# A stated task order in place of a greedy list scheduler, in a fused recurrent-attention and feed-forward kernel

## The chip, the core and the metric

The kernel runs on one core of a Trainium2 chip. The metric is the device time of the whole program in microseconds; three runs are shown for the kernel before, and beside them one profiled execution whose records the rows below come from. In the records PE is TensorE, DVE is VectorE, ACT is ScalarE, POOL is GpSimd and SP is SyncE, which issues all loads and stores.

## The reference

The first half is a gated linear recurrence over 768 steps for 4 batches and 8 heads of 48 columns; the second is a feed-forward block on the result, with token shift, squared ReLU and a sigmoid gate. Everything is float32.

```python
f = 1 / (1 + exp(-f_logit))
for t in range(S):                       # per batch and head; state is D x D
    state = f[t, :, None] * state + outer(k[t], v[t])
    y[t] = q[t] @ state
x = y, heads side by side                # (B, S, 384)
xk = mu_k * x + (1 - mu_k) * x_prev      # x_prev: x shifted by one step
xr = mu_r * x + (1 - mu_r) * x_prev
k = relu(xk @ w_k);  v = (k * k) @ w_v;  r = sigmoid(xr @ w_r)   # 384 -> 1024 -> 384
out = r * v
```

## The kernel before

The recurrence is cut into 24 chunks of 128 steps (N; six per batch), the feed-forward block into 8 units of three chunks (U). Every piece of work is a task with a short name, and the program is a list of tasks. For chunk i they are: loads `qk` and `v` (SP); `b`, a scan on DVE that multiplies the gates up; `bl`, its last column; `ln` and `rb` (ACT), the reciprocal; `q`, `n`, `kr`, `k`, which scale queries and keys; `TR`, four transposes of k on PE, and `kt`, their copy out of PSUM; `SP`, 32 small matmuls for the scores and then up to 32 for the state sums; `m`, the mask on the scores (for chunk 0 a copy on ACT, then `mg` on POOL); `g`, `za`, `zb`, `T`, which carry the state; `YA` and `YB`, the output matmuls, with `w`, a short wait between them; and `y`, the copy of the result into x.

For unit u they are: `sp` (six small transfers that spread two heads over free partitions of x), `x0`, `d`, `xm`, `xh`, `xl` (token shift, then the split of a float32 into a high part and a remainder, for keys n=0 and gate n=1 and three row blocks each); `F`, eight groups of nine matmuls with w_k; `r`, `h`, `kk`, `l` (ReLU, square, and its split); `R`, three groups of nine with w_r; `lg` and `sg` (the gate); `W`, six groups of twelve with w_v; `o` and `out`. All 1,368 matmuls of F, R and W are on line 505, and each product is made of three. `F0.0` needs `xl0.00` to `xl0.02`; every F, R and W follows the one before it.

The weights come as 64-bit words in 18 pieces (8 of `wk`, 4 of `wr`, 6 of `wv`), and each is turned into float32 by three DVE instructions (`S`, `T`, `X` at lines 623, 634 and 637), a cast on ACT (`H`) and a subtraction (`L`). Later the pieces are read once more for a check (`c`, `cm`, then `lo`, `lot`, `lom`, `strong`), which chooses a general path that does not run on these inputs.

PSUM holds four rotating buffers `pm`, which b, TR, d, F, R, W and the weights' S share, and two fixed tiles: `pss` for scores and sums, `py` for outputs. SBUF buffers rotate too (`BUFS`).

What sets the order: `Plan.schedule` is a greedy list scheduler. It runs on the host when the program is built; every task has a guessed duration for each engine that may take it, a `place` (a due time), and a DMA has a guess of its own. In turn it takes the task that can start first, and emits it; `emit` pins each engine's instructions to that order, so every engine works strictly down its list. Where PE would be without work by the guesses, after an early part, `fill` puts in small matmuls of the identity into an unused part of `py` (line 702). Constants hold some work back: `TIED` and `BUNDLE` keep YA behind the next chunk's kt and q, and YB behind the next chunk's SP; `late` and `behind` hold loads; `DEAR` makes DVE and ACT look dearer than POOL where there is a choice.

```python
near = I("kt", i + 1) + I("q", i + 1) + I("m") + I("T") if BUNDLE and TIED <= i < N - 1 else []
pl.add(f"SP{i}", at, ("P", 0.8 if cs < NCH - 1 else 0.62, 0, scores_sums),
       after=I("q") + I("kt") + I("m", i - 1) + I("zb", i - 1) + I("T", i - 1), uses=[("ktk", i), ("v", i)])
```

Of the kernel before, what the change touches and what calls it, by code (L numbers as in the profile page):

```python
# [59 lines left out]
class Plan:  # L60

    def __init__(self):
        self.tasks, self.users = {}, defaultdict(list)
        self.filler = None

    def add(self, name, place, *ways, after=(), takes=(), uses=()):
        assert name not in self.tasks, name  # L70
# [12 lines left out]

    def schedule(self, trace=None):
        free = {"P": 0.0, "V": 2.2, "A": 0.0, "G": 1.0, "Q": 0.7}
        wire, under = 0.0, [0.0] * 8
        last_p = "F"
        read = 0.0
        end, slot = {}, {}
        slots = {tag: [(0.0, i) for i in range(n)] for tag, (n, _) in BUFS.items()}  # L90
        left = {b: len(u) for b, u in self.users.items()}
        last = defaultdict(float)
        waits = {n: set(t[3]) for n, t in self.tasks.items()}
        for b, us in self.users.items():
            taker = [n for n in us if b in self.tasks[n][4]]
            assert len(taker) == 1, (b, taker)
            for n in us:
                if n != taker[0]:
                    waits[n].add(taker[0])
        then = defaultdict(list)  # L100
        for n, w in waits.items():
            for m in w:
                assert m in self.tasks, (n, m)
                then[m].append(n)
        ready = {n: () for n, w in waits.items() if not w}
        way_of = {}
        order = []
        while ready:
            best = None
            for n, names in ready.items():  # L110
                _, place, ways, _, takes, _ = self.tasks[n]
                at = 0.0
                if any(not slots[b[0]] for b in takes):
                    continue
                for b in takes:
                    at = max(at, min(slots[b[0]])[0])
                at = {w[0]: max([at] + [0.0 if way_of[m] == w[0] else end[m] for m in names]) for w in ways}
                pick = min(((max(at[w[0]], free[w[0]]) + w[1] + DEAR.get(w[0], 0.0), w) for w in ways), key=lambda x: x[0])[1]
                start = max(at[pick[0]], free[pick[0]])
# [2 lines left out]
                if best is None or k < best[0]:
                    best = (k, n, start, pick)
            assert best, "no order: " + ", ".join(sorted(ready))
            _, n, start, way = best
            _, _, _, _, takes, uses = self.tasks[n]
            e, us, port, _ = way
            if e == "P" and self.filler and "cst" in end:

                t = max(free["P"], read, FILL[0])  # L130
                stop = t + (start - t - 0.25) * FILL[1]
                cold = t + 6.0 if last_p == "F" else 0.0
                while t + (us4 := 1.76 if t < cold else 0.88) < stop:
                    name = f"fill{len(order)}"
                    fw = "P", 0.88, 0, lambda: self.filler(4)
# [1 line left out]
                    order.append((name, fw, slot))
                    if trace is not None:
                        trace.append((name, "P", t, t + us4))
                    free["P"] = t = t + us4  # L140
                    last_p = "FILL"
            if e == "Q":

                for _ in range(port):
# [802 lines left out]
```

## Time and profile before

| | |
|---|---|
| three runs | 359.09, 359.39, 360.88 us (median 359.39) |
| span of the profiled execution, first to last instruction | 361.0 us |
| PE busy | 329.9 us, 4514 matmuls |
| DVE busy | 262.8 us, 528 instructions |
| ACT busy | 200.3 us |
| POOL busy | 195.0 us |
| DMA | 45.32 MB |

The profiled execution has no time of its own beside the span, so the span is set against the runs directly: it is 1.6 us above their median. Busy time is a sum over the whole span; what an engine waits for is read from a stretch. In the records one instruction's end can overlap the next one's start on the same engine, so a sum over a queue is better made from start to start.

### The profile page before, as it was taken

How to read it: one execution, taken by the hardware profiler on the slowest of the kernel's cores; microseconds unless marked ns; L12 is line 12 of the kernel's file. 1: busy time of each engine (PE TensorE's matmuls, PEld its weight loads, DVE VectorE, ACT ScalarE, POOL GpSimd, SP SyncE). 2: the span in 40 equal slices, each digit the busy share in tenths (PEclk: the TensorE clock that was granted, in tenths of full speed). 3: DMA queues.
4: the chain of work that ended last, by engine and by line, in shares of the span. 5: the costliest groups of instructions: out<-in, count | busy, mean ns of one | idle time of the engine just before them, and what ended most of it. 6: DMA issues, size and time to landing. Idle time of an engine off the chain costs nothing.

```text
span 361.0 us, 10931 instructions
## 1 busy us (share of the span) xinstructions
PE 329.9 (91%) x4514; PEld 315.1 (87%) x4514; DVE 262.8 (73%) x528; ACT 200.3 (55%) x398; POOL 195.0 (54%) x235
## 2 busy tenths in 40 slices
PE   0496689988999999999999999999999999999993
PEld 0385589878989999999999999999999989999993
DVE  7979668989988988986998678948964852733210
...
PEclk9999667999999999999999999999999999999998
...
GB/s 283 405 334 190 246 142 82 83 107 129 182 185 137 27 117 285 165 200 183 245 139 49 141 193 165 0 50 95 105 80 36 50 26 6 14 44 22 3 24 51
DMA packets 20650, 45.32 MB, mean 126 GB/s; under 512 B 2928, under 2 KB 13040, under 8 KB 20592
## 3 DMA queue, kind: packets, MB, share of 16 engines
q1 hardware_dynamic: 20592, 44.55, 37.6%
q8 instruction: 37, 0.61, 0.7%
...
## 4 chain that ended last, share of the span: by engine, by line
PE 84%; DVE 7%; POOL 2%; issue 2%; DMA 2%; ACT 1%; DVEq 0%; ACTq 0%
PE pm L505 64%; PE py L362 8%; PE pss L325 4%; PE pm L310 4%; PE py L702 3%; PE pss L345 3%; DVE pm L240 2%; DMA words<-in_wv 1%; DVE pm L634 1%; POOL wk L644 1%; DVE pm L623 1%; DMA lg<-in_wr 1%; POOL wv L644 1%; DVE qk L250 1%; POOL k2l L543 1%
## 5 line engine op out<-in xcount | busy, mean ns | idle before, releaser
L505 PE MATMUL pm<-xh,wk 128*128 128x384 f32 x384 | 105.2, 345 | 1.6 <-POOL wk L644 1.4
L505 PE MATMUL pm<-wv,k2h 128*128 128x384 f32 x384 | 98.8, 338 | 0.0
L543 POOL TENSOR_TENSOR k2l<-kk,k2h 128x384 fp32r<-128x384 f32 x64 | 67.8, 1062 | 35.1 <-DVE kk L535 18.2
L497 POOL TENSOR_TENSOR xl<-xm,xh 128x384 fp32r<-128x384 f32 x48 | 52.1, 1088 | 52.1 <-DVE xh L491 40.7
L505 PEld LDWEIGHTS pm<-xh,wk 128*128 128x128 f32 x384 | 70.1, 189 | 4.2 <-POOL wk L644 2.8
L505 PEld LDWEIGHTS pm<-wv,k2h 128*128 128x128 f32 x384 | 68.8, 188 | 0.2
L505 PE MATMUL pm<-xl,wk 128*128 128x384 f32 x192 | 64.8, 338 | 0.0
L505 PE MATMUL pm<-wv,k2l 128*128 128x384 f32 x192 | 64.5, 336 | 0.0
L528 ACT ACTIVATE r<-pm 128x384 f32<-128x384 f32 x55 | 26.9, 489 | 31.7 <-PE pm L505 30.8
L505 PE MATMUL pm<-wr,xh 128*128 128x384 f32 x144 | 37.9, 344 | 1.4 <-DVE words L637 1.4
L535 DVE SCALAR_TENSOR_TENSOR kk<-pm,r 128x384 f32<-128x384 f32 x39 | 21.7, 556 | 22.0 <-ACT r L528 21.3
L505 PEld LDWEIGHTS pm<-xl,wk 128*128 128x128 f32 x192 | 36.2, 189 | 0.0
L505 PEld LDWEIGHTS pm<-wv,k2l 128*128 128x128 f32 x192 | 36.1, 188 | 0.0
L533 ACT ACTIVATE k2h<-r 128x384 fp32r<-128x384 f32 x64 | 33.6, 525 | 4.0 <-DVE r L529 1.4
L595 DVE TENSOR_TENSOR o<-pm,lg 128x384 f32<-128x384 f32 x24 | 13.3, 554 | 30.4 <-PE pm L505 30.3
L240 DVE TENSOR_TENSOR_SCAN pm<-f,low 128x512 f32<-128x512 f32 x24 | 33.9, 1414 | 0.0
L702 PE MATMUL py<-ident 128*128 128x64 f32 x104 | 17.9, 347 | 14.3 <-DVE pm L240 14.3
L702 PEld LDWEIGHTS py<-ident 128*128 128x128 f32 x104 | 17.5, 260 | 14.5 <-issue 14.3
L362 PEld LDWEIGHTS py<-qk,z 64*64 64x64 f32 x704 | 17.2, 142 | 13.4 <-issue 7.1
L362 PE MATMUL py<-qk,z 64*64 64x64 f32 x704 | 23.7, 238 | 5.7 <-DVE z L296 2.3
L394 ACT ACTIVATE x<-py 64x128 f32<-64x128 f32 (+1 forms) x51 | 15.8, 310 | 23.3 <-PE py L362 22.5
L505 PEld LDWEIGHTS pm<-wr,xh 128*128 128x128 f32 x144 | 25.3, 188 | 2.0 <-DVE words L637 1.5
...
## 6 DMA issues: line engine op xcount, KB each, us to landing
...
```

Source lines behind the costliest of these rows:

```text
L240: pl.add(f"b{i}", ga, ("V", 1.25, 1, lambda: nc.vector.tensor_tensor_scan(b().rearrange(FL), f().rearrange(FL), self.low.rearrange(FL), 1. ...
L310: nc.tensor.transpose(pk()[:, j], k()[:, j], self.ident)
L325: nc.tensor.matmul(self.pss[HALF[h], r, 64 * j : 64 * j + 64], k()[HALF[r], j, HALF[h]], q()[HALF[r], j, HALF[h ^ j % 2]], start=True, sto ...
L362: first[c, h] = nc.tensor.matmul(to, lhs, rhs, start=(c, h) not in first, stop=stop, skip_group_check=True)
L394: e.activation(o, i_, AF.Copy, scale=-1.0)
L497: e.tensor_tensor(lo(), xm(), hi().bitcast(F32), op=ALU.subtract)
L505: nc.tensor.matmul(ps, lhs(a, j), rhs(bb, j), start=ends[0] and i == 0, stop=ends[1] and i == len(pr) - 1)
L528: pl.add(f"r{u}.{f}", kf, ("A", 0.5, 0, lambda r=r, ps=ps: nc.scalar.activation(r(), ps(), AF.Relu)), ("V", 0.56, 0, lambda r=r, ps=ps: nc ...
L533: pl.add(f"h{u}.{f}", kf, ("A", 0.53, 0, lambda r=r, hi=hi: nc.scalar.activation(hi(), r(), AF.Square)), after=[f"r{u}.{f}"], **kw)
L535: pl.add(f"kk{u}.{f}", kf, ("V", 0.56, 0, lambda r=r, ps=ps, kk=kk: nc.vector.scalar_tensor_tensor(kk(), ps(), 0.0, r(), op0=ALU.max, op1= ...
L543: e.tensor_tensor(lo(), kk(), hi().bitcast(F32), op=ALU.subtract)
L702: self.nc.tensor.matmul(self.py[:, 0, 256:320], self.ident, self.ident[:, :64], start=False, stop=True, skip_group_check=True)
```

## The change

`Plan.schedule` with its guessed durations and due times goes, and with it the constants and the fillers. A text, `ORDER`, names all 1,382 tasks in one sequence; a suffix names the engine where a task may run on more than one. `stated` walks through it, gives out buffers in the order in which the sequence frees them, and `emit` pins each engine to it as before. The instructions of each task are the same, but which engine takes an `l`, `xl`, `xh`, `kk`, `kr`, `za`, `kt`, `y` or `L` can differ. `SP` becomes `S` (scores, behind q, k and the mask of the chunk before) and `P` (sums, behind kt, zb and T). YA and YB lose the ties to the next chunk, loads lose `late` and `behind`. At the head the sequence begins with the first gate block and the scan b0, where the kernel before begins with four pieces of w_r.

```diff
-LEAD, GATE, PREP = 1.669, 0.274, 0.51
-WORDS = {"wk": (-0.282, 0.023), "wr": (-4.892, 0.005), "wv": (-0.241, 0.052)}
-HAND, DRAIN = 0.136, 0.465
-TURN = {(True, False): 0.125, (False, True): 0.2}
-TIED = 8
-FILL = (14.0, 0.85)
-LATE = {"sp": 3.3, "qk": 1.9}
-BUNDLE = True
 AWAY = 1
-SPLIT = True
 HALVED = 1
-PLACE = {"f1": -0.627, "f2": 0.21, "sf2": -1.016, "qk0": 0.854, "qk1": -0.278, "qk2": 0.127, "qk3": 0.31, "v0": -0.151, "v1": -0.224, "cst": 0.482, "mu": 0.138, "f3": -1.807}
-CHECK = (2.0, 0.2)
-DEAR = {"V": 2.498, "A": 2.512}
+ORDER = """
+f0.0 sf0.0 b0 bl0/V f0.1 sf0.1 b1 f0.2 sf0.2 f1 b2 wr0 wrS0 mu wrT0 wrX0 qk0 sf1 onemu b3 ex ln0 rb0 kr0/G q0 n0 bl1/A
+g2 ln1 qk1 q1 qk3 rb1 kr1/G q3 n1 ln3 rb3 bl3/A qk2 ln2 rb2 k0 cst k1 g1 n3 q2 kr3/G k3 TR0 S0 v0 kt0/A P0 TR1 bl2/A
+n2 m0 zb0/A wk0 wkS0 b4 YA0 w0/A kr2/G k2 S1 mg0 YB0 wkT0 ln4 kt1/A T0 za1/G g3 y0/A v1 m1 wkX0 P1 wk2 wr1 v2 TR2 wkS2
+rb4 kt2/A wv0 zb1 b5 T1 wvS0 wkT2 x00 YA1 wkH0 wrH0 bl4/A w1/A ln5 YB1 y1/A P2 wvT0 wkX2 wkH2 wv1 za2/G wrL0/G S2
+wkL2/G wkL0/G TR3 wvX0 kt3/A zb2 YA2 m2 S3 w2/A YB2 rb5 wrS1 wk6 wkS6 wrT1 wr2 f2 wkT6 wrX1 T2 za3/G wkX6 wvS1 wrS2
+qk4 kr4/G wvH0 wvL0/G wvT1 wrT2 v3 P3 y2/A qk5 kr5/G q4 wrX2 wvX1 sf2 wvH1 wvL1/G n4 m3 k4 g4 sp0.2 sp0.0 d0.00 xm0.00
+d0.12 zb3 YA3 d0.02 xm0.12 xm0.02 bl5/A xh0.00/A wk1 sp0.1 d0.01 wrH1 w3/A xh0.02/A S4 TR4 YB3 xl0.00/G wrL1/G xm0.01
+xl0.02/G xh0.01/A kt4/A wrH2 xl0.01/G wkS1 wk3 wkS3 d0.10 wkT1 wkT3 wkX1 wkH1 wkX3 wkH3 wkL1/G wkL3/G wrL2/G wk4 wk5
+wk7 wkS4 T3 wkT4 xm0.10 F0.0 wkH6 wkX4 y3/A x01 wkL6/G q5 n5 d0.11 xm0.11 k5 F0.1 wkS7 v5 r0.0/A kk0.0/A wv3 v6 v4 wr3
+h0.0 l0.0/G wkH4 r0.1/A kk0.1/A wkL4/G za4/G g5 wkS5 h0.1 l0.1/G F0.2 r0.2/A h0.2 wkT7 wv2 qk6 kk0.2/A l0.2/G wkT5
+wkX7 F0.3 r0.3/A wkX5 wkH5 wkL5/G wvS3 wrS3 wvT3 kk0.3/A h0.3 l0.3/G wkH7 xh0.10/A xl0.10/G P4 zb4 wvX3 wrT3 T4 za5/G
+wrX3 F0.4 r0.4/A TR5 YA4 xh0.11/A kk0.4/A kt5/A wvH3 F0.5 w4/A h0.4 m4 wrH3 wvS2 wkL7/V r0.5/A b6 wrL3/V xh0.12/A wvT2
+wvL3/G ln6 xl0.11/G P5 S5 kk0.5/A q6 xl0.12/G rb6 bl6/A l0.4/V kr6/G f3 wvX2 h0.5 wvH2 wvL2/G YB4 y4/A F0.6 F0.7 R0.0
+n6 k6 TR6 zb5 YA5 l0.5/G m5 S6 r0.6/A r0.7/A h0.7 kk0.6/A kk0.7/A kt6/V h0.6 lg0.0/A P6 zb6/A w5/V YB5 y5/A R0.1 R0.2
+wv5 wvS5 wvT5 wvX5 wvH5 YA6 lg0.1/A b7 qk7 lg0.2/A v8 wv4 wvS4 wvT4 wvX4 q7 g7 sp1.0 W0.00 m6 w6/A wvH4 wvL4/V l0.6/G
+YB6 l0.7/G sp1.1 d1.1 xm1.01 wvL5/G W0.01 W0.10 xm1.11 d1.0 xm1.00 sp1.2 qk8 v7 xh1.00/V xl1.00/V c2 bl7/A ln7 rb7
+xm1.10 n7 kr7/G W0.11 xh1.10/V k7 sg0 o0.0 y6/A d1.2 xm1.02 o0.1 b8 T6 c4 out0.1 xh1.02/A sf3 xh1.01/A ln8 rb8
+xl1.01/G W0.20 W0.21 v9 qk9 xl1.02/V F1.0 bl8/V xm1.12 kr8/V r1.0/A q8 o0.2 n8 kk1.0/V k8 F1.1 F1.2 r1.1/A h1.0
+kk1.1/V TR7 kt7/A F1.3 S7 P7 l1.0/V xh1.11/V b9 r1.2/A h1.1 kk1.2/V za7/G zb7 m7 TR8 xh1.12/A h1.2 kt8/V T7 l1.1/G
...
+W6.11 o6.1 out6.1 W6.20 W6.21 o6.2 out6.2 F7.0 r7.0/A h7.0 F7.1 F7.2 kk7.0/V l7.0/G r7.1/A h7.1 kk7.1/V l7.1/G r7.2/A
+F7.3 F7.4 h7.2 kk7.2/V l7.2/G r7.3/A h7.3 kk7.3/V l7.3/G F7.5 F7.6 F7.7 r7.4/A h7.4 kk7.4/V l7.4/G r7.5/A h7.5 kk7.5/V
+l7.5/G r7.6/A h7.6 kk7.6/V l7.6/G r7.7/A h7.7 kk7.7/V l7.7/G R7.0 R7.1 lg7.0/A R7.2 W7.00 W7.01 W7.10 W7.11 lg7.1/A
+lg7.2/A sg7 o7.0 out7.0 o7.1 W7.20 out7.1 W7.21 o7.2 out7.2
+"""
...
-        self.filler = None
...
-    def schedule(self, trace=None):
...
-                stay = BUNDLE and pick[0] == "P" and last_p[0] in "SY" and n[0] in "FRWT"
-                k = (round((start + 0.2 * stay) / 0.15), place, n)
...
-            if e == "P" and self.filler and "cst" in end:
-
-                t = max(free["P"], read, FILL[0])
-                stop = t + (start - t - 0.25) * FILL[1]
-                cold = t + 6.0 if last_p == "F" else 0.0
-                while t + (us4 := 1.76 if t < cold else 0.88) < stop:
-                    name = f"fill{len(order)}"
-                    fw = "P", 0.88, 0, lambda: self.filler(4)
-                    self.tasks[name] = (name, 0.0, (fw,), (), (), ())
...
+    def stated(self, order):
+
+
+        slot, left = {}, {b: len(u) for b, u in self.users.items()}
+        free = {tag: list(range(n)) for tag, (n, _) in BUFS.items()}
+        done, out = set(), []
+        for word in order.split():
+            name, _, e = word.partition("/")
+            _, ways, after, takes, uses = self.tasks[name]
+            way = next(w for w in ways if w[0] == e) if e else ways[0]
+            assert done.issuperset(after) and all(b in slot for b in uses), name
             for b in takes:
+                slot[b] = free[b[0]].pop(0)
             for b in (*takes, *uses):
                 left[b] -= 1
                 if not left[b]:
+                    free[b[0]].append(slot[b])
+            done.add(name)
+            out.append((name, way, slot))
+        assert done == set(self.tasks), set(self.tasks) - done
+        return out
...
-        late = [f"sp{i // UC - 2}.{KJ - 1}"] if i >= 2 * UC and c == 0 else []
-        pl.add(f"qk{i}", ga - 0.3, ("Q", 1.42, 1, lambda: nc.sync.dma_start(self.qk_t[i % NQ], self.qkt[i])),
-               after=I("SP", i - NQ) + I("TR", i - NQ) + I("YB", i - NQ) + late)
-        pl.add(f"v{i}", at - 0.3, ("Q", 0.52, 1, lambda: nc.sync.dma_start(self.b("v", i), self.vt[i])),
-               after=late, takes=[("v", i)])
+        pl.add(f"qk{i}", ("Q", lambda: nc.sync.dma_start(self.qk_t[i % NQ], self.qkt[i])),
+               after=I("S", i - NQ) + I("TR", i - NQ) + I("YB", i - NQ))
+        pl.add(f"v{i}", ("Q", lambda: nc.sync.dma_start(self.b("v", i), self.vt[i])),
+               takes=[("v", i)])
...
-        def scores_sums():
-            scores()
-            sums()
-
-        pl.add(f"SP{i}", at, ("P", 0.8 if cs < NCH - 1 else 0.62, 0, scores_sums),
-               after=I("q") + I("kt") + I("m", i - 1) + I("zb", i - 1) + I("T", i - 1), uses=[("ktk", i), ("v", i)])
+        pl.add(f"S{i}", ("P", scores), after=I("q") + I("k") + I("m", i - 1))
+        pl.add(f"P{i}", ("P", sums), after=I("kt") + I("zb", i - 1) + I("T", i - 1), uses=[("ktk", i), ("v", i)])
         first = {}
...
-        near = I("kt", i + 1) + I("q", i + 1) + I("m") + I("T") if BUNDLE and TIED <= i < N - 1 else []
-        pl.add(f"YA{i}", at, ("P", 0.22, 0, lambda: y_state(1)), after=I("za") + I("zb") + I("q") + I("y", i - 1) + near)
-        pl.add(f"w{i}", at, ("A", 0.16, 0, lambda: nc.scalar.copy(self.done, self.py[:, :, 192])),
-               ("V", 0.15, 0, lambda: nc.vector.tensor_copy(self.done, self.py[:, :, 192])), after=I("YA"))
-        pl.add(f"YB{i}", at, ("P", 0.66, 0, y_own), after=I("mg" if i < AWAY else "m") + I("w") + (I("SP", i + 1) if TIED <= i < N - 1 else []), uses=[("ss", i), ("v", i)])
+        pl.add(f"YA{i}", ("P", lambda: y_state(1)), after=I("za") + I("zb") + I("q") + I("y", i - 1))
+        pl.add(f"w{i}", ("A", lambda: nc.scalar.copy(self.done, self.py[:, :, 192])),
...
-                pl.add(f"sf{u}", -1.0 if SPLIT and u == 2 else -9, ("A", 1.5 + 2.6 * (SPLIT and u == 2), 0, sf),
-                       after=[f"f{u}", ("ex" if SPLIT else "sf1") if u > 1 else "sf0.2"])
+                pl.add(f"sf{u}", ("A", sf),
+                       after=[f"f{u}", "ex" if u > 1 else "sf0.2"])
             else:
...
-            behind = ["qk5"] if not clamp and (name == "wk" and p >= 4 or name == "wv" and p >= 1) else []
-            pl.add(f"{name}{p}", place - 0.4, ("Q", n * P * 8 / 370e3, 1, lambda: nc.sync.dma_start(view(), load())),
-                   after=behind, **tu)
+            pl.add(f"{name}{p}", ("Q", lambda: nc.sync.dma_start(view(), load())),
+                   **tu)
...
-    def fill(self, count):
-
-        for _ in range(count):
-            self.nc.tensor.matmul(self.py[:, 0, 256:320], self.ident, self.ident[:, :64], start=False, stop=True, skip_group_check=True)
-
...
-    k.emit(plan.schedule())
+    k.emit(plan.stated(ORDER))
```

## Rows read from the trace of the kernel before

**Rows 1.** The page: granted clock, and DMA rate, in 40 slices of the span.

```profile
PEclk9999667999999999999999999999999999999998
GB/s 283 405 334 190 246 142 82 83 107 129 182 185 137 27 117 285 165 200 183 245 139 49 141 193 165 0 50 95 105 80 36 50 26 6 14 44 22 3 24 51
```

**Rows 2.** Three stretches: length; busy PE, PEld, DVE, ACT, POOL; clock, DMA share, GB/s.

```profile
3.60:57.35 53.75, 34.89 (x760) 31.93 (x760) 43.67 (x93) 26.94 (x53) 24.75 (x36) 0.85 0.75 259
57.35:102.76 45.41, 42.54 (x464) 39.22 (x460) 41.73 (x75) 31.45 (x64) 34.52 (x35) 0.99 0.45 140
102.76:142.00 39.24, 39.20 (x575) 37.46 (x576) 35.88 (x73) 22.86 (x46) 26.04 (x30) 1.00 0.40 132
```

**Rows 3.** The chain that ended last: start us, us, what.

```profile
0.75 2.83 DMA lg<-in_wr
...
102.76 1.77 PE pm L505 x9
...
303.49 51.93 PE pm L505 x297
355.45 0.56 DVE o L595
```

**Rows 4.** Timeline of DVE, single instructions of the kinds in the sum.

```profile
9.03 1.70 DVE L240 TENSOR_TENSOR_SCAN pm<-f,low 128x512 f32<-128x512 f32 x1
...
20.61 0.68 DVE L250 TENSOR_TENSOR qk<-qk,pm 128x512 f32<-128x512 f32 x1
21.20 0.55 DVE L315 COPY ktk<-pm 128x384 f32<-128x384 f32 x1
21.67 1.22 DVE L240 TENSOR_TENSOR_SCAN pm<-f,low 128x512 f32<-128x512 f32 x1
22.93 0.16 DVE L244 COPY bl<-pm 128x4 f32<-128x4 f32 x1
...
59.23 0.56 DVE L623 TENSOR_SCALAR pm<-words_k2l 128x384 int32<-128x384 int32 x1
...
64.20 0.69 DVE L623 TENSOR_SCALAR pm<-words 128x512 int32<-128x512 int32 x1
...
66.26 0.56 DVE L623 TENSOR_SCALAR pm<-words_k2h 128x384 int32<-128x384 int32 x1
...
95.68 0.41 DVE L262 SCALAR_TENSOR_TENSOR qk<-pm,qk 128x256 f32<-128x256 f32 x1
...
96.41 0.55 DVE L595 TENSOR_TENSOR o<-pm,lg 128x384 f32<-128x384 f32 x1
```

**Rows 5.** Groups of DVE's instructions by shape.

```profile
L482 DVE SCALAR_TENSOR_TENSOR xm<-pm,mu_sb,x 128x384 f32<-128x384 f32 x42 | 25.7, 613 | 0.7
```

**Rows 6.** The page's groups: count, busy us, mean ns, idle before and releaser.

```profile
L497 POOL TENSOR_TENSOR xl<-xm,xh 128x384 fp32r<-128x384 f32 x48 | 52.1, 1088 | 52.1 <-DVE xh L491 40.7
L528 ACT ACTIVATE r<-pm 128x384 f32<-128x384 f32 x55 | 26.9, 489 | 31.7 <-PE pm L505 30.8
L535 DVE SCALAR_TENSOR_TENSOR kk<-pm,r 128x384 f32<-128x384 f32 x39 | 21.7, 556 | 22.0 <-ACT r L528 21.3
L702 PE MATMUL py<-ident 128*128 128x64 f32 x104 | 17.9, 347 | 14.3 <-DVE pm L240 14.3
```

**Rows 7.** Timeline of PE: start us, us, line, operation, tiles.

```profile
46.82 7.49 PE L702 MATMUL py<-ident 128*128 128x64 f32 x40
...
57.35 0.69 PE L505 MATMUL pm<-xh,wk 128*128 128x384 f32 x1
```

**Rows 8.** Timeline of SP: the six transfers of the first spread.

```profile
38.31 5.27 SPq L452 DMA_DIRECT2D x<-stage  x6
```

**Rows 9.** PE in stretches of 2 us: length, busy (instructions), granted clock, DMA.

```profile
36.00:38.00 2.00, 0.33 (x2) 1.00 0.95 288
...
50.00:52.00 2.00, 2.00 (x12) 0.50 0.04 12
...
58.00:60.00 2.00, 2.00 (x12) 0.87 0.75 190
```

More of the change, by code (lines that the diff above doesn't have):

```diff
@@ L77, in in_order @@
         turn = defaultdict(int)
-        for name, _, ways, _, takes, _ in self.tasks.values():
+        for name, ways, _, takes, _ in self.tasks.values():
             for b in takes:
@@ L82, in in_order @@
             yield name, ways[0], slot
-    def schedule(self, trace=None):
[L85 to L119, printed above, removed]
-                stay = BUNDLE and pick[0] == "P" and last_p[0] in "SY" and n[0] in "FRWT"
-                k = (round((start + 0.2 * stay) / 0.15), place, n)
[L122 to L127, printed above, removed]
-            if e == "P" and self.filler and "cst" in end:
-                t = max(free["P"], read, FILL[0])
-                stop = t + (start - t - 0.25) * FILL[1]
-                cold = t + 6.0 if last_p == "F" else 0.0
-                while t + (us4 := 1.76 if t < cold else 0.88) < stop:
-                    name = f"fill{len(order)}"
-                    fw = "P", 0.88, 0, lambda: self.filler(4)
-                    self.tasks[name] = (name, 0.0, (fw,), (), (), ())
[L137 to L144, printed above, removed]
-                    start = max(start, under[-8]) + (0.6 if n[:2] in ("sp", "wk") else 0.42)
-                    wire = max(wire, start + LATE.get(n[:2], 1.3)) + us / port
-                    under.append(wire + 0.3)
-                done, free[e] = wire + 0.3, start
-            else:
-                if e == "P":
-                    us += TURN.get((last_p[0] in "FRWTl", n[0] in "FRWTl"), 0.0)
-                    last_p = n
-                if port and free["G"] > start:
-                    us += min(us, (free["G"] - start) / 2)
-                free[e] = start + us
-                done = start + us + (DRAIN if e == "P" else 0.0)
-            end[n], way_of[n] = done + HAND, e
-            if n[0] == "y" or n[0] == "w" and n[1].isdigit():
-                read = max(read, end[n])
@@ L162, in schedule @@
-                slots[b[0]].remove(s)
-                slot[b] = s[1]
+                slot[b] = free[b[0]].pop(0)
             for b in (*takes, *uses):
                 left[b] -= 1
-                last[b] = max(last[b], done)
                 if not left[b]:
-                    slots[b[0]].append((last[b] + HAND, slot[b]))
-            order.append((n, way, slot))
-            if trace is not None:
-                trace.append((n, e, start, start + us))
-            del ready[n]
-            for m in then[n]:
-                waits[m].discard(n)
-                if not waits[m]:
-                    ready[m] = self.before(m)
@@ L177, in schedule @@
-        assert len(end) == len(self.tasks) - sum(n.startswith("fill") for n in self.tasks), [n for n in self.tasks if n not in end][:20]
-        return order
-    def before(self, n):
-        _, _, _, after, takes, uses = self.tasks[n]
-        out = list(after)
-        for b in uses:
-            out += [m for m in self.users[b] if b in self.tasks[m][4]]
-        return [m for m in out if m != n]
+                    free[b[0]].append(slot[b])
+            done.add(name)
+            out.append((name, way, slot))
@@ L756, in emit @@
             at = len(done)
-            way[3]()
+            way[1]()
             for ins in done[at:] if pinned else ():
```

217 lines of the change are left out of this document (124 added, 93 removed).

## The prediction

> **What bounds the kernel now.** I read the slices of the page first, then the stretches, the chain, and PE's and DVE's timelines. The granted clock is full but for three slices, 36 to 63 us [rows 1]. The stretches split the run in two. Until 57.35 us, where F0.0 starts, PE is busy 34.9 of 53.8 us, part of that with fillers; DVE has 43.7 busy. From 57.35 to 102.76 us DVE is busy 41.7 of 45.4 us, and from 102.76 us PE is busy without a break, 39.20 of 39.24 us in the first stretch [rows 2]. The chain says the same: from F1.0 at 102.76 us it runs on PE, and the last 297 matmuls take 51.93 us, or 174.8 ns each, ending at 355.42 us [rows 3]. So the end is F1.0's start, plus what PE still has to do, plus a tail of 361.0 - 355.42 = 5.6 us. Whatever the new order wins must come before F1.0, or out of the little that PE loses after it.
>
> **What PE has left at F1.0.** Before, it takes 355.42 - 102.76 = 252.7 us for 1,197 matmuls of line 505 (1,368 less the 171 of unit 0), which are 1,197 x 0.1748 = 209.2 us, and 17 chunks' outputs with 16 chunks' TR and SP. The rest, 43.5 us, is about 2.55 us a chunk with all turns and waits [rows 3]. The new order has at F1.0 one TR, one S and one P more to do; I take half a chunk, 1.3 us. From F6.5 on both orders have the same 297 matmuls of line 505 and nothing else on PE. So the new end is F1.0 + 252.7 + 1.3 + 5.6 = F1.0 + 259.6 us.
>
> **When F1.0 can start.** In the new text the last DVE task named ahead of F1.0 is xl1.02, the 132nd of DVE's list. DVE works strictly down the list, so F1.0 waits for all 132. From start to start they cost [rows 4]:
> - 54 word instructions. The first 12 filled 3.58 to 9.03 us (the load of w_r lands at 3.58 us [rows 3]): 5.5. Nine for w_k took 64.20 - 59.23 = 4.97 us, so 24 take 13.3. Three for w_v took 2.06 us, so 18 take 12.4. Together 31.2.
> - 9 scans b at 22.93 - 21.67 = 1.26 us: 11.3.
> - 22 passes over 512 columns (8 q, 8 n, 6 m) at 21.20 - 20.61 = 0.59: 13.0.
> - 8 k, three instructions each, at 96.41 - 95.68 = 0.73: 5.8.
> - 11 xm at 0.61 [rows 5]: 6.7.
> - 14 of about 384 columns (d, xh, xl, l, kt, o, L) at 0.55, between the copy's step of 0.47 and the word instruction with its wait: 7.7.
> - 11 of 192 columns (zb, T), half a 512 pass: 3.3; three tiny ones, 0.3.
>
> That is 79.3 us. DVE now begins with b0, which needs the first third of the first gate block and a sigmoid over it. That load is the first on the queue and about as large as the w_r piece that landed at 3.58 us; with 0.7 us for the sigmoid (DVE's pass over as many columns is 0.68) and 0.1 for handing on, b0 starts at 4.4 us instead of 9.03.
>
> The unknown is how long DVE idles in its list. The lower bound is nothing. The upper one is what it idles now over the same part: 99.2 us less 43.7 and 41.7 busy [rows 2], 13.8 us. I take 6: the word instructions, which DVE has few of in hand while it waits for the spread now, stand in the new text between the steps of chunks 1 to 4, but a fixed list cannot step past a late load or a late copy. F1.0 = 4.4 + 79.3 + 6 + 0.3 for the last hand-on = 90.0 us, 12.8 earlier than now.
>
> One dearer price is in the rows: the scan at 9.03 us took 1.70 us and the one at 21.67 us 1.22 [rows 4]; at 1.70 all nine would add 4 us, which lies inside the idle's bounds. The Trainium skill (GPSIMD Engine Reference, Key points) says that GpSimd shares its SBUF interfaces with VectorE and contends with its instructions of two SBUF inputs; by that all nine could be the dear kind.
>
> **The loads.** Ahead of qk0 stand two gate blocks and one w_r piece, 1.9 MB, and with it 2.4 MB; the first two slices moved 283 and 405 GB/s [rows 1], 2.55 MB by 9 us, and DVE asks for qk0 after 7.2 us of its list, at 11.6 us. The first w_k piece is behind 4.7 MB, there by about 14.5 us, and is asked for near 18. So I charge nothing; what is late sits in the 6 us.
>
> **The fillers.** 104 of them take 17.9 us of PE [rows 6], almost all while PE waits for something else, so their removal is worth little. The 40 from 46.82 to 54.31 us [rows 7] end just before matmuls that could have begun perhaps 1 to 2 us sooner. That is nothing in the sum, because DVE's list sets F1.0. What they cover is the clock, a rival below.
>
> **F0.0, and PE ahead of F1.0.** By the same prices DVE's first 60 tasks, up to xm0.01, are 36.6 us: 4.4 + 36.6 = 41.0, then xh, 0.5, and xl on POOL, 1.1 [rows 6], some hand-ons and 2 us of the idle: F0.0 at about 45 us, where it is 57.35 now [rows 7]. The spread that feeds it took 5.27 us of SP's queue [rows 8]; in the new text it stands behind y2, with sf2 on ACT in between, and DVE has words and chunk 3 to do meanwhile. From 45 to 90 us PE has unit 0 (171 matmuls, 29.9 us) and 2.7 chunks (6.9): 36.8 of 45 us, at full clock. That cover is 8 us; without it PE is late.
>
> **S and P apart.** Same matmuls. Thirteen of the 24 pairs are no longer neighbours, so some turn between large and small matmuls is added; it is inside the 2.55 us a chunk, and the ties that are lifted work the other way. Nothing.
>
> **After F1.0.** From F1.0 to F2.0 the new list holds 37.2 us of DVE (same prices) beside 38.5 of PE, and 34.0 beside 37.6 to F3.0. DVE was at 35.9 of 39.2 there before, without a PE wait [rows 2]. The margin is 1.3 us in the first and 3.6 in the second, so I take nothing, and up to 5 us as the bound.
>
> **Sum.** 90.0 + 252.7 + 1.3 + 5.6 = 349.6 us of span, 11.4 below 361.0. The span shown is 1.6 us above the median of the runs, so the median should be 348. Without idle it is 342, with all of it 355.8, with the late waits too 360.8.
>
> **The rivals.**
> 1. *The idle stays, and the fixed lists wait after F1.0 as well.* 13.8 us of idle and 1 to 2 us of new waits: 355.8 + 1.5 = 357.3, faster by 0.6%. For it: both lists are nearly full until F3.0. Against: the word instructions fill what DVE waited for.
> 2. *The order is no better than the old one.* F1.0 near 101.5 us: 359.5, within 0.5%, which is about what a measurement of this kernel can tell from no change. For it: PE waits for almost nothing after 82 us now. Against: the 79.3 us of DVE's list do not reach 101.5.
> 3. *The clock falls, and F0 runs at half level.* It was at half in slices before F0.0 though PE was busy throughout (50 to 52 us), had fallen after a stretch with 0.33 of 2 us busy, and rose at 58 to 60 us, after F0.0 had begun [rows 9]. Without fillers PE enters F0.0 colder. If the half level held through all of unit 0, 36.8 us would become 73.6, F1.0 would be at 45 + 73.6 = 118.6 us and the median at 376.6: slower. It decides against the change when over 53% of that work is slow (45 + 36.8 x 1.53 = 101.5). Against it: dense matmuls brought the level up within 2 us of F0.0 before, and a part below 22% fits in the 8 us of cover. The Trainium skill (TensorE: Matmul & The Clock Gate, HAM oscillation) warns that a PE that waits between bursts falls back to the throttled clock each time; the fall near 38 us agrees. By that rule alone the 376.6 would stand.
> 4. *The list stalls PE within each unit.* F waits for one of four pm buffers, which r and kk give back: 0.49 + 0.56 us and two hand-ons, about 1.25 [rows 6], under one F group of 1.57. One scan ahead of kk on DVE, 1.26 us, breaks that by 0.9. If 16 of the 64 groups were so hit, 15 us: 363, slower; it decides from about 12 hits. Against: the old order has the same buffers and waits for none.
>
> **Chances.** Forecast (342 to 355.8) 0.70; rival 1, 0.10; rival 2, 0.07; rival 3, 0.08; rival 4, 0.05. So faster by over 0.5% is 0.80, within it 0.07, slower 0.13. The range, 341 to 358.5, holds the forecast and rival 1; what is left out is rivals 2 to 4.
>
> **What the next profile would show.** Right: b0 near 4.4 us, F0.0 near 45 and F1.0 near 90; DVE without a wait over 1.5 us ahead of F1.0; F1.0 to the last W in about 254 us. Wrong: granted clock at half beyond F0.2 or so; PE waits for kk or words of over 5 us in all after F1.0; a DVE wait for the spread or for w_k pieces of several us. A search on guessed times could have put one late load where everything stands behind it; that would break the 6 us first.

## The result, and the profile after

The changed kernel takes 348.5 us (median of four runs, 347.79 to 350.27), where the kernel before took 359.83 beside it: a ratio of 0.9693, with an interval of 0.9656 to 0.973. The profiled execution took 350.27 us, the longest of the four, and its span is 348.4 us, 12.6 below the 361.0 of before. In every execution of these kernels the time is 1.7 to 2.1 us above the span of the same execution, so the 361.0 of before belongs to one of about 363 us, some 3 above its kernel's median; between the medians the gain is 11.3 us. One execution of e7, the profiled one, was in a slow state (355.29 us, the other four 346.62 to 347.96), so e7 has no starts in the table below.

The slices of the page show the clock and the load rate (as [rows 1] did before):

```profile
PEclk9998699999999999999999999999999999999998
GB/s 228 383 390 98 149 336 145 198 105 221 179 129 213 87 123 3 134 220 140 178 87 116 230 189 253 86 83 24 193 8 35 47 24 15 5 45 24 2 24 53
```

Only two slices, 26 to 44 us, show a 6 or an 8, where [rows 1] has three below 9; no filler is there to hold the clock up. The stretches that answer to [rows 2], with the same columns:

```profile
3.60:45.00 41.40, 17.72 (x544) 15.04 (x548) 36.03 (x75) 29.38 (x63) 21.34 (x30) 0.88 0.74 257
45.00:90.00 45.00, 42.34 (x538) 39.71 (x531) 44.17 (x86) 35.24 (x80) 29.11 (x31) 1.00 0.62 206
90.00:128.00 38.00, 37.17 (x625) 35.80 (x625) 32.09 (x71) 21.57 (x44) 17.29 (x24) 1.00 0.42 138
```

The head is 11.4 us shorter up to F0.0, PE has lost half of its 34.9 us there (fillers among it), and from 45 to 90 us DVE and PE are now both nearly full: 44.2 and 42.3 of 45 us. From the timeline of DVE, its first scan, two steps of word instructions, and the end of its list ahead of F1.0:

```profile
4.30 1.23 DVE L211 TENSOR_TENSOR_SCAN pm<-f,low 128x512 f32<-128x512 f32 x1 [1.65 <-ACT f L381]
...
43.47 0.56 DVE L581 TENSOR_SCALAR pm<-words_k2l 128x384 int32<-128x384 int32 x1
43.94 0.55 DVE L590 SCALAR_TENSOR_TENSOR pm<-words_k2h,pm 128x384 int32<-128x384 int32 x1
44.40 0.56 DVE L590 SCALAR_TENSOR_TENSOR pm<-words_k2l,pm 128x384 int32<-128x384 int32 x1
...
58.42 2.33 DVE L211 TENSOR_TENSOR_SCAN pm<-f,low 128x512 f32<-128x512 f32 x1
...
84.34 1.05 DVE L460 TENSOR_TENSOR xl<-xm,xh 128x384 fp32r<-128x384 f32 x1
```

From the timeline of PE, the wait ahead of F0.0, F0.0, R0.0, and F1.0 (in [rows 7] F0.0 started at 57.35):

```profile
41.30 0.71 PE L329 MATMUL py<-qk,z 64*64 64x64 f32 x16 [7.05 <-ACT pm L437]
...
45.94 0.44 PE L468 MATMUL pm<-xh,wk 128*128 128x384 f32 x1 [0.57 <-DVE words_k2l L593]
...
64.50 0.62 PE L468 MATMUL pm<-wr,xh 128*128 128x384 f32 x2 [1.67 <-DVE words L593]
...
85.77 0.34 PE L468 MATMUL pm<-wv,k2l 128*128 128x384 f32 x1
85.95 0.33 PE L468 MATMUL pm<-xh,wk 128*128 128x384 f32 x1
```

And the end of the chain of waits, which answers to [rows 3]:

```profile
290.73 51.93 PE pm L468 x297
...
342.68 0.56 DVE o L555
```

F1.0 starts at 85.95 instead of 102.7 us, 16.8 earlier. The last W ends at 342.66, 256.7 us after F1.0, where it was 252.7. So the head gave 16.8 us and the part after it took 4.0 back.

What the head gave can be read from DVE. The first line is the kernel before, from its first word instruction to F1.0; the second is the changed kernel, from its first scan to the end of xl1.02 (columns as in [rows 2]):

```profile
3.58:102.76 99.18, 77.43 (x1220) 71.16 (x1220) 85.40 (x168) 58.39 (x117) 59.26 (x70) 0.91 0.61 205
4.30:85.39 81.09, 55.45 (x1044) 50.14 (x1045) 75.90 (x150) 62.70 (x138) 50.09 (x60) 0.94 0.66 227
```

Before, DVE was busy for 85.4 us and idle for 13.8; now it is busy for 75.9 and idle for 5.2. Of the 18.1 us by which the stretch is shorter, 9.5 are less work on DVE and 8.6 are less idle; less 0.7 for the later start and 0.6 from xl1.02 to F1.0, that is the 16.8. The smaller work comes only in part from the sequence. Of the tasks that both orders name ahead of F1.0, 27 stand on another engine now: y2, y5, three kt, six xh and six bl went from DVE to ACT, for instance, and six subtractions came from POOL to DVE. No run keeps the old engines in the new sequence, so how much of the gain each of the two gives is not shown.

### The profile page after: what moved, and what is told of

Same layout as the page of the kernel before. It is cut to its first block, busy times and chain, and to the rows that moved or that the text cites. A ratio compares the mean times of both kernels' runs of the same rounds, so it can differ in the third digit from the quotient of the medians.

```text
span 348.4 us, 10719 instructions
## 1 busy us (share of the span) xinstructions
PE 310.7 (89%) x4410; PEld 296.7 (85%) x4410; DVE 253.7 (73%) x521; ACT 205.3 (59%) x431; POOL 168.0 (48%) x209
## 4 chain that ended last, share of the span: by engine, by line
PE 65%; DVE 15%; DMA 6%; issue 5%; ACT 3%; SPq 2%; POOL 2%; DVEq 0%; ACTq 0%; POOLq 0%
PE pm L468 55%; PE py L329 5%; DMA qk<-in_qkt 2%; PE pss L296 2%; DMA x<-stage 2%; PE pm L281 2%; DMA words<-in_wv 2%; DVE pm L590 1%; PE pss L316 1%; POOL k2l L505 1%; DVE pm L581 1%; DVE xm L445 1%; DVE pm L211 1%; DVE pm L428 1%; SPq L199 1%
## 5 line engine op out<-in xcount | busy, mean ns | idle before, releaser
L505 POOL TENSOR_TENSOR k2l<-kk,k2h 128x384 fp32r<-128x384 f32 x57 | 59.2, 1049 | 43.6 <-ACT k2h L495 25.6
L460 POOL TENSOR_TENSOR xl<-xm,xh 128x384 fp32r<-128x384 f32 x42 | 45.9, 1103 | 65.4 <-ACT xh L453 43.9
L490 ACT ACTIVATE r<-pm 128x384 f32<-128x384 f32 x53 | 25.9, 491 | 32.2 <-PE pm L468 31.9
L211 DVE TENSOR_TENSOR_SCAN pm<-f,low 128x512 f32<-128x512 f32 x24 | 33.0, 1375 | 6.0 <-ACT ktk L285 3.7
L495 ACT ACTIVATE k2h<-r 128x384 fp32r<-128x384 f32 x64 | 32.8, 522 | 6.0 <-DVE r L491 4.6
L497 DVE SCALAR_TENSOR_TENSOR kk<-pm,r 128x384 f32<-128x384 f32 x33 | 18.2, 555 | 19.3 <-ACT r L490 16.3
L281 PE MATMUL pm<-ident,qk 128*128 128x128 f32 x96 | 16.1, 294 | 16.2 <-DMA words_k2h<-in_wk 16.2
L229 POOL TENSOR_TENSOR qk<-qk,rb 128x256 f32<-128x256 f32 x21 | 16.3, 775 | 29.3 <-ACT bl L214 16.1
L329 PE MATMUL py<-qk,z 64*64 64x64 f32 x704 | 22.8, 235 | 8.4 <-ACT pm L437 7.0
L329 PEld LDWEIGHTS py<-qk,z 64*64 64x64 f32 x704 | 16.8, 140 | 14.8 <-ACT pm L437 7.2
L281 PEld LDWEIGHTS pm<-ident,qk 128*128 128x128 f32 x96 | 12.2, 149 | 17.2 <-DVE qk L237 16.2
```

The source lines that it names most:

```text
L211: pl.add(f"b{i}", ("V", lambda: nc.vector.tensor_tensor_scan(b().rearrange(FL), f().rearrange(FL), self.low.rearrange(FL), 1.0, op0=ALU.mu ...
L229: e.tensor_tensor(k()[:, ::2], k()[:, ::2], rb()[:, ::2], op=ALU.mult)
L281: nc.tensor.transpose(pk()[:, j], k()[:, j], self.ident)
L329: first[c, h] = nc.tensor.matmul(to, lhs, rhs, start=(c, h) not in first, stop=stop, skip_group_check=True)
L460: e.tensor_tensor(lo(), xm(), hi().bitcast(F32), op=ALU.subtract)
L490: pl.add(f"r{u}.{f}", ("A", lambda r=r, ps=ps: nc.scalar.activation(r(), ps(), AF.Relu)), ("V", lambda r=r, ps=ps: nc.vector.tensor_scalar ...
```

## The experiments

Each kernel below is the changed one with its text `ORDER`, or a task beside it, edited. "Last W" is the end of the last 297 matmuls. F0.0 to span are those of one profiled execution, the median and the ratio are over all executions. Medians of the kernel before, measured beside them, were 360.33 us (e1 to e4), 360.41 (e5 to e8) and 360.92 (e9 to e12).

| run | F0.0 | F1.0 | F1.0 to last W | span | median | ratio and interval |
|---|---|---|---|---|---|---|
| before | 57.35 | 102.7 | 252.7 | 361.0 | 359.83 | |
| changed | 45.94 | 85.95 | 256.7 | 348.4 | 348.5 | 0.9693 (0.9656 to 0.973) |
| e1 new head, old rest | 45.73 | 86.97 | 262.3 | 354.8 | 357.11 | 0.992 (0.9891 to 0.995) |
| e2 old head, new rest | 52.93 | 98.40 | 263.2 | 367.4 | 369.58 | 1.0279 (1.024 to 1.0317) |
| e3 old order, stated | 54.25 | 99.96 | 253.3 | 358.9 | 360.53 | 1.0011 (0.9984 to 1.0039) |
| e4 fillers ahead of y2 | 52.36 | 92.42 | 255.2 | 353.1 | 356.05 | 0.9895 (0.9864 to 0.9926) |
| e5 as e1, joint mended | 43.83 | 85.53 | 252.6 | 343.8 | 347.44 | 0.9647 (0.9589 to 0.9706) |
| e6 as e2, joint mended | 54.11 | 100.05 | 255.1 | 360.7 | 361.95 | 1.0057 (1.0026 to 1.0087) |
| e7 fillers behind y2 | | | | | 347.65 | 0.9635 (0.9576 to 0.9694) |
| e8 w_r at the head | 44.76 | 84.10 | 256.2 | 345.8 | 348.95 | 0.9699 (0.9634 to 0.9764) |
| e9 changed, again | 46.05 | 86.07 | 255.9 | 347.6 | 349.0 | 0.9686 (0.9637 to 0.9735) |
| e10 e5, again | 43.69 | 85.52 | 252.7 | 343.8 | 347.48 | 0.9641 (0.9593 to 0.969) |
| e11 S beside P | 47.98 | 88.09 | 265.1 | 358.7 | 359.54 | 0.9951 (0.9921 to 0.9981) |
| e12 eight more on DVE | 45.00 | 92.38 | 255.8 | 353.7 | 355.44 | 0.9856 (0.9812 to 0.99) |

### e1 and e2: which half of the order does it

e1 keeps the new sequence up to F1.0 and takes the rest in the sequence of the kernel before; e2 is the other way round.

```diff
-xl1.01/G W0.20 W0.21 v9 qk9 xl1.02/V F1.0 bl8/V xm1.12 kr8/V r1.0/A q8 o0.2 n8 kk1.0/V k8 F1.1
+x02 TR7 xh1.11/V kt7/A xl1.11/G f4 S7 P7 bl8/V g8 q8 o0.2 F1.0 m7 out0.2 kr8/G zb7 T7 YA7
```

> The new order up to F1.0, then the old order (SP split into S and P) for all that is left; no fillers. Theory (the gain is made ahead of F1.0, by DVE's list): F1.0 near 86 us as in the changed kernel, then PE needs what it needed before, 252.7 + 1.3 us, and 5.6 of tail: a span near 345.5, some 3 us below the changed kernel. Rival (the gain is spread over the whole order, or comes from lifting the ties in the dense part): 352 us or more.

> The old order up to F1.0 without fillers, then the new order for what is left. Theory: F1.0 near 102 us, then 256.7 us as in the changed kernel and 5.7 of tail: a span near 364, no gain at all. Rival (the gain is in the dense part): 350 us or less.

The F1.0 starts came out about as the head theory has them: 86.97 with the new head, 98.40 with the old. The ends did not: both theories missed the span, 354.8 for 345.5 and 367.4 for 364. In the waits of PE after F1.0, e1 has one item that counts:

```profile
PE pm L468 <- DVE o L555: 7.9, 1, 7.9
```

It is an artefact of the joint. In both kernels the loads for the check (`c`) stand in another sequence, and at the joint they come to stand behind `words` buffers that are not yet free; the loads queued behind them on SP are late. In e1, DVE stands at 119.02 and 123.85 us for two of these loads, 5.7 and 4.1 us, with the `o` that PE waits for behind them in its list. In e2 the same thing made PE wait 5.7 us for a `v`. So these two runs say where F1.0 lies and nothing about the rest.

### e5 and e6: the same with the joint mended

```diff
-sp2.1 k11 W1.01 sp2.2 cm2 c0 cm0 c1 cm1 qk12 W1.10 c3 d2.0 xm2.00
+sp2.1 k11 W1.01 cm4 sp2.2 cm0 qk12 W1.10 c7 c11 d2.0 xm2.00
```

> As e1, with the check's loads in the new order's sequence, so that none stands in a queue behind a buffer that is taken. Theory (the gain is made ahead of F1.0, and the old order is worth the same or a little more after it): without the 7.9 us that PE lost in e1, a span near 346, 2 to 3 us below the changed kernel. Rival (the old order after F1.0 needs the old head's lead in stored work): 350 or more.

> As e2, with the check's loads in the old order's sequence. Theory: F1.0 near 101 us, then some 256 us and the tail, a span near 361, as before the change. Rival (the new order after F1.0 gains by itself): 355 or less.

In e5 the checks take the pieces in the sequence of the new order (c2, c4, c0, c7, ...; the lines show one place of some twenty), in e6 in that of the old one; all else is e1 and e2. With the joint mended, the head alone gives all of the gain: 347.44 us, and F1.0 at 85.53. The new rest alone gives none: 361.95 us, slower by 0.57% with an interval that leaves out no change. The old rest took 252.6 us from F1.0, the new one 255.1. That settles the place of the gain, ahead of F1.0. The old rest of e5 still has TR7, S7 and P7 ahead of F1.0, so 1.3 us of its lead over the changed kernel is work that was done earlier. With the same tasks left, e6 needs 255.1 us and e3, below, 253.3: behind F1.0 the new order is some 2 us dearer.

### e3: the old order without fillers and without the scheduler

```diff
-f0.0 sf0.0 b0 bl0/V f0.1 sf0.1 b1 f0.2 sf0.2 f1 b2 wr0 wrS0 mu wrT0 wrX0 qk0 sf1 onemu b3
+wr0 wr1 wr2 wr3 f0.0 f0.1 f0.2 wrS0 qk1 wrT0 v0 wrX0 f1 wrS1 v1 wrH0 wrT1 qk2 wrL0/G wrX1
```

> The old order of all tasks as a stated list, S and P next to each other, fillers left out. Theory (fillers fill waits and delay little): F1.0 1 to 2 us earlier than before, span 358 to 361. Rival 1 (their 17.9 us of PE stand in the way): 343 to 350. Rival 2 (they hold the clock up): F0 runs longer at half level and the span is above 363.

360.53 us against 360.33: no change. Its F1.0, 99.96, is 2.7 earlier than in the profile of before, but its span is 2.1 shorter too, and the executions of the kernel before that were measured beside it had spans of 356.3 to 361.0 us, most of them below 360; so this 2.7 cannot be told from the spread between executions. Taking the fillers and the scheduler away is worth nothing that can be measured; what the new text states, sequence and engines together, is.

### e4 and e7: fillers put back

Eight tasks of four filler matmuls each, named behind P3, where PE waits 7.05 us in the changed kernel; in e7 they are named one task later, behind y2.

```diff
-wvT1 wrT2 v3 P3 y2/A qk5
+wvT1 wrT2 v3 P3 fill0 fill1 fill2 fill3 fill4 fill5 fill6 fill7 y2/A qk5
```

> The changed kernel with 32 fillers put on PE after P3, where PE waits 7 us for the spread. Theory (F0.0 waits for DVE's word instructions, not for PE, and runs at full level anyway): no change, 348.4 us within 1. Rival (the clock costs something at F0 in the changed kernel): 2 us or more faster. If the fillers end late: up to 1 us slower.

> As e4, with the 32 fillers named after y2, so that y2 does not wait for them; on PE they run in the same place, in the 7 us in front of YA3. Theory (they cover a wait, and F0.0 runs at full level without them): no change against the changed kernel, 348.4 us within 1. Rival (YA3 to YB3 at half level cost something ahead of F0.0): 1 to 2 us faster.

e4 is 7.5 us slower than the changed kernel, where the theory had no change. Its PE and ACT rows (each filler shows as two records, so the 32 are x64 here and the 104 of [rows 6] are 52):

```profile
32.44 7.36 PE L657 MATMUL py<-ident 128*128 128x64 f32 x64
...
52.36 0.44 PE L468 MATMUL pm<-xh,wk 128*128 128x384 f32 x1 [0.80 <-DVE words_k2l L593]
```

```profile
39.90 0.97 ACT L360 ACTIVATE x<-py 128x256 f32<-128x256 f32 x3 [8.98 <-PE py L657]
```

The fillers write the tile `py`, and y2, the copy out of it, waits until the last of them has ended: 39.90 instead of 33.72 us, 6.2 late. F0.0 is 6.4 late with it and F1.0 6.5. The clock is at full level at F0.0 here, as it is without fillers. So F0.0 hangs on y2 and what follows it, not on the clock: 6.2 us of delay on y2 are 6.4 of F0.0. In e7, where y2 no longer waits, the time is that of the changed kernel.

What follows y2 is read from ACT and SP in the changed kernel:

```profile
33.72 0.97 ACT L360 ACTIVATE x<-py 128x256 f32<-128x256 f32 x3 [3.23 <-PE py L329]
34.72 0.28 ACT L360 ACTIVATE stage<-py 128x128 f32<-128x128 f32 x1
35.01 1.28 ACT L387 ACT_TABLE_LOAD   x1
36.31 1.48 ACT L387 ACTIVATE f<-f 128x1536 f32<-128x1536 f32 x1
37.81 1.28 ACT L389 ACT_TABLE_LOAD   x1
39.10 0.65 ACT L596 CAST wv<-words 128x512 fp32r<-128x512 f32 x1
39.65 1.59 ACT L437 ACTIVATE pm<-x,mu_sb 128x384 f32<-128x384 f32 x3
```

```profile
35.02 2.50 SPq L417 DMA_DIRECT2D x<-stage  x4
```

ACT works without a pause from y2 to d0.00 at 39.65 us. Between them stand sf2 with a table load on either side of it, 4.1 us, and a cast. The transfers for d0.00 are the last two of the four; the last is issued at 36.9 us and, at the 1.9 us that the median of these transfers takes to landing, is there near 38.8. So d0.00 waited for ACT's own list, and without sf2 in that place it could have started up to 0.9 us earlier. No run moved sf2. From d0.00 the delay goes on through DVE's list: xm0.00 waits for d0.00, and F0.0 for a word instruction that stands behind it.

### e8: w_r back at the head

The four loads of w_r and their twelve word instructions go to the front, as in the kernel before; everything else keeps its sequence.

```diff
-f0.0 sf0.0 b0 bl0/V f0.1 sf0.1 b1 f0.2 sf0.2 f1 b2 wr0 wrS0 mu wrT0 wrX0
+wr0 wr1 wr2 wr3 wrS0 wrT0 wrX0 wrS1 wrT1 wrX1 wrS2 wrT2 wrX2 wrS3 wrT3 wrX3 f0.0 sf0.0 b0 bl0/V
```

> The changed kernel with the four w_r loads and their twelve DVE instructions put back at the head of the lists, as before the change. DVE's list up to F1.0 has the same 132 entries. Theory of the list (the sum ahead of F0.0 and F1.0 counts): F0.0 later by the one w_r piece that now stands ahead of it, 1.4 us, F1.0 the same within 1, span 348 to 350. Rival of the chain (what counts is when b0 starts, for all of chunks 0 to 2 and the spread hang on it): everything 4.5 us later, span 352 to 353.

b0 starts at 9.13 us, 4.8 later, and F0.0 and F1.0 come 1.2 and 1.9 us *earlier*. In the first microseconds DVE has word instructions where the changed kernel waits for the sigmoids. The changed kernel's waits of DVE ahead of F1.0:

```profile
DVE pm L211 <- ACT f L381: 2.1, 2, 1.7
DVE xm L440 <- ACT pm L437: 1.7, 1, 1.7
DVE sm L273 <- PE pss L296: 1.2, 1, 1.2
DVE pm L581 <- DMA lg<-in_wr: 1.0, 1, 1.0
```

In e8 the first and the third are gone. The time, 348.95 us, doesn't differ. Neither forecast of F0.0 came, 1.4 us later or 4.5 us later. But an early b0 is not what won: DVE must do the twelve instructions somewhere ahead of F1.0, and what counts is its whole list with its waits.

### e9 and e10: the best version against the changed kernel

e9 is the changed kernel and e10 the kernel of e5, both on one chip.

```diff
-F1.0 bl8/V xm1.12 kr8/V r1.0/A q8 o0.2 n8 kk1.0/V
+F1.0 m7 out0.2 kr8/G zb7 T7 YA7 n8 za8/G r1.0/A
```

> The changed kernel once more, as the measure for the other three on the same chip: 0.969 of before within its interval.

> The kernel of e5 once more. Theory (from F1.0 to the last W the old order needs 252.6 us and the new one 256.7): 2 to 4 us below the changed kernel in the same call. Rival (the difference is that of two single executions): the same within 1 us.

In the profiles e10 is 3.8 us shorter, 343.8 against 347.6; F1.0 to the last W takes 252.7 against 255.9. In the medians it is 1.5 us, 347.48 against 349.0, and the intervals overlap. The new head with the old rest beats the kernel before for certain; that it beats the changed kernel is likely (e5's ratio, 0.9647 beside other runs of the kernel before, lies on the same side) and not settled. e10 also entered F0.0 at half level, 0.69 us for its first matmul, and lost nothing by it that shows in F1.0.

### e12: eight more instructions on DVE ahead of F1.0

Eight products of 512 columns into a tile that nothing reads, behind m6; the rest of the computation is untouched.

```diff
-W0.00 m6 w6/A wvH4
+W0.00 m6 extra0 extra1 extra2 extra3 extra4 extra5 extra6 extra7 w6/A wvH4
```

> The changed kernel with eight more products of 512 columns on DVE (of constants, into a tile of their own) after m6, between F0.0 and F1.0: 4.8 us at 0.6 each. Theory (DVE's list sets F1.0; it ends 0.6 us before F1.0 now): F1.0 later by 4.2 us and the end by as much, less what the dense part takes up. Rival (PE sets F1.0): less than 1 us.

The eight took 6.58 us and not the 4.7 that eight steps of 0.59 [rows 4] would make. Most of their steps are 0.72; two are 1.14, while POOL scaled keys beside them (74.29 to 76.50 us). F1.0 came 6.3 later than in e9 and the last W 6.2. So what is put on DVE's list here comes out at the end. That it comes out at nearly its own length is in part chance: some of it is taken up, and the clock adds to the rest. The second row shows how it gets there, through a wait of PE for the weights of W:

```profile
73.37 6.58 DVE L658 TENSOR_TENSOR extra<-low 128x512 f32<-128x512 f32 x8
```

```profile
80.61 0.69 PE L468 MATMUL pm<-wv,k2h 128*128 128x384 f32 x1 [5.09 <-DVE wv L600]
```

The stretches of e12 behind that wait (length; busy PE, PEld, DVE, ACT, POOL; clock, DMA share, GB/s):

```profile
74.00:80.00 6.00, 1.52 (x42) 1.12 (x36) 5.76 (x9) 5.91 (x7) 2.21 (x2) 0.84 0.39 128
80.00:84.00 4.00, 3.39 (x11) 3.39 (x12) 3.83 (x8) 0.62 (x3) 0.00 (x0) 0.50 0.58 176
84.00:88.00 4.00, 4.00 (x22) 4.00 (x21) 3.96 (x10) 0.00 (x0) 0.00 (x0) 0.89 0.22 88
```

After the 5.1 us PE is busy for 3.39 us at half level, 1.2 GHz, and for 4 us at 0.89: 3.39 x 0.5 + 4 x 0.11 = 2.1 us more. 5.1 + 2.1, less the 1.05 by which F0.0 was earlier here, is 6.2, beside the 6.3 of F1.0.

### e11: scores and sums side by side again

Each S goes to stand directly ahead of its P, at the place of the later of the two. In five chunks (1, 18, 19, 21, 22) the mask m, which needs S, stood between them and had to go behind S, and so it stands between S and P.

```diff
-k2 S1 mg0 YB0 wkT0 ln4 kt1/A T0 za1/G g3 y0/A v1 m1 wkX0 P1 wk2
+k2 mg0 YB0 wkT0 ln4 kt1/A T0 za1/G g3 y0/A v1 wkX0 S1 m1 P1 wk2
```

> The changed kernel with each S moved to its P, or P to its S, whichever comes later, so that all 24 pairs are neighbours again; five masks come later for it. Theory (two tasks are worth nothing by themselves): the changed kernel's time within 1.5 us. Rival (the split lets scores start before the copy kt, which shortens the chain of chunks 0 to 3): F0.0 later by 1 us or more and 2 us or more slower.

359.54 us: 10.5 more than e9, of the 11.9 by which e9 is below the kernel before. The theory that the split is worth nothing missed by far, in this form of the test. F0.0 is 1.9 and F1.0 2.0 later, by as much as the rival said: S1, which e9 has at 20.8 us ahead of YB0, stands behind YB0 here and starts at 23.70, P1 behind m1 starts 0.7 later than in e9, and y2 at 35.60 instead of 33.75 us. From F1.0 to the last W it takes 265.1 us for e9's 255.9, another 9.2 (between these two profiles; between the medians it is 10.5 in all). Waits of PE there, and the two that stand for them in its timeline:

```profile
PE pss L316 <- issue: 2.9, 2, 2.0
PE py L329 <- ACT done L347: 1.1, 4, 0.3
PE pss L316 <- ACT x L360: 0.9, 1, 0.9
PE pss L316 <- DVE ss L308: 0.8, 1, 0.8
```

```profile
228.48 0.57 PE L316 MATMUL pss<-v,ktk 64*48 64x48 f32 x32 [0.81 <-DVE ss L308]
...
241.18 0.57 PE L316 MATMUL pss<-v,ktk 64*48 64x48 f32 x32 [2.00 <-issue]
```

There are four such waits, at 228.48, 241.18, 268.67 and 290.82 us: P18, P19, P21 and P22, 0.81 + 2.00 + 0.86 + 0.86 = 4.5 us. Each P starts 0.05 to 0.11 us after the end of its chunk's mask product on DVE (240.40 + 0.68 = 241.08 for the one at 241.18), so that the two waits that the view puts down to "issue" and the one that it puts down to ACT are the same wait. Scores and sums are two column ranges of one tile, `pss`; P waits for the mask that reads the other range. After the 2.00 us the clock was 0.57 over the next 4 us, which is another 4 x 0.43 = 1.7. All waits of PE behind F1.0 are 6.9 us here and 1.3 in e9, so that 5.6 + 1.7 = 7.3 of the 9.2 are located.

All four stand where m is named between S and P. At the other chunks behind F1.0, where P follows S at once, no wait of P shows. So behind F1.0 most of what the run prices is the order S, m, P without other work between. Plain neighbours are priced by e5 and e10: from chunk 7 on all their pairs stand side by side with no mask between, PE has no wait behind F1.0, and their 252.6 and 252.7 us are the shortest of the table. There "nothing" holds.

## Why the prediction came out as it did

**The forecast and its sum.** 348.0 was forecast and 348.5 measured. The cause that was named, DVE's list ahead of F1.0, is the one that the runs show: e5 and e6 place the gain there, and e12 shows that more on the list makes the end later. The terms did not hit as closely as their sum; that the sum is within 0.5 us is partly luck. In the order of the prediction:

- *b0 at 4.4 us.* 4.30 measured.
- *132 DVE tasks, 79.3 us, and 6 us of idle.* From 4.30 to the end of xl1.02 at 85.39 are 81.1 us for the 85.3 of the sum. Of these 5.2 are idle (4.4 in four waits: 0.5 for a sigmoid, 1.0 for w_r, 1.2 for PE, 1.7 for d0.00; the 1.65 for the first sigmoid lies ahead of b0), so the 6 was nearly right. One wait, the 1.7, is over the 1.5 that was named as a sign. The term that was mis-sized is the list: 75.9 and not 79.3. Its 54 word instructions, priced at 31.2, took about 27 from start to start. Word instructions of two pieces that alternate step by 0.46 us (43.94 to 44.40) where the row that I took, of instructions that each need the one before, steps by 0.55 [rows 4].
- *The scan's dear price.* Of nine scans two were dear, 2.33 and 1.58 us, both with subtractions on POOL beside them; the median was 1.23. By the Trainium skill (GPSIMD Engine Reference, Key points) all nine could have been. The trace shows some 1.5 us in all, not the 4 of nine dear ones: POOL was idle when six of the nine began, and the scan at 19.75 took 1.22 with a product on POOL beside it.
- *F0.0 at about 45.* 45.94 measured. But the reason given was DVE's list alone, with the spread covered. DVE did wait 1.68 us for d0.00 and PE 7.05 us, and e4 shows that a delay on y2 passes into F0.0 in full. The chain y2, sf2, d0.00 on ACT binds F0.0 together with DVE's list; the spread ran beside sf2.
- *F1.0 at 90.0, set by DVE, with 8 us of cover for PE.* 85.95 measured, 4.0 earlier; PE's cover was gone. F1.0 follows the last W of unit 0 directly, 0.56 us after xl1.02 was ready. From F0.0 to F1.0 PE took 40.0 us for the 36.8 predicted, with some 2 us of waits. The last of them is R0.0's, 1.67 us for a word instruction of DVE that ends at 64.45 us; from 64.50 to F1.0 PE works without a wait. So DVE's list sets F1.0 by where R0.0 can start, and PE's own work does the rest. DVE still decides, as e12 shows, because it also feeds the weights of W0.
- *F1.0 to the last W, 252.7 + 1.3.* 256.7 measured, 2.7 too little; 255.9 in e9. The 1.3 for the extra TR, S and P is in it; the waits of PE in that part were 1.8 us in all (the longest, 0.8 at 121.69, for an xm behind the spread sp2), which lie in the bound of 5 that was kept for it.
- *Tail 5.6.* 5.7. *Span to median, minus 1.6.* Plus 0.1. The 1.6 was no property of the kernel: a time is 1.7 to 2.1 us above its own span, and the profiled execution of before was some 3 us above its kernel's median, that of the changed kernel 1.8.

So -4.0 ahead of F1.0, +2.7 behind it and +1.7 for the execution make the 0.5.

**The fillers.** "Worth little" holds: e3 without them and e7 with some show no change. **The loads.** Nothing, as said: DVE waited 1.0 us for the first w_r piece. **S and P apart.** "Nothing" was too simple. For neighbours without a mask between it holds behind F1.0 (e5, e10). In the head the new places of S and P are worth 1.9 us of y2 (e11, where m1 stands between S1 and P1). And a P directly behind its mask waits for it, 0.8 to 2.0 us, which was not seen, though scores and sums lie in one tile. The prediction's total was hardly touched, because the new sequence puts work between: in e9 one P waits 0.9 us behind F1.0, in the changed kernel one 0.5.

**The rivals.** Of the 13.8 us of idle 5.2 stayed (rival 1), and the order was better (rival 2). The list hardly stalled PE within a unit (rival 4): after F1.0 no wait for kk is listed, and one of 0.8 us for an xm, which reads a pm buffer. The clock (rival 3) did not fall for long in the changed kernel: the granted clock was 0.50 from 41 to 45 us, behind the 7.05 us wait, and F0.0 ran at full level at 45.94, 0.44 us for the first matmul. But its mechanism is there. In e12 and e11 waits of 5.1 and 2.0 us were followed by 2.1 and 1.7 us of loss. The Trainium skill (TensorE: Matmul & The Clock Gate, HAM oscillation) says that waits between bursts bring the throttled clock each time; these two traces agree, for several microseconds after the wait and not for a whole unit, and so the 376.6 that the rule alone would have given was far off. Nor did each wait do it: behind R0.0's 1.67 us the clock stayed at 1.00.

**What stays open.** How much of the gain is the sequence and how much the choice of engines has not been separated. The new rest is some 2 to 3 us dearer than the old one beyond the extra chunk work; waits of PE are 1.0 to 1.9 us of it, and the rest is not located. Some 1.9 us of e11's loss behind F1.0 are not located. Whether e10 really beats the changed kernel would need more runs.
